# First MoE's output product by seven block products per batch in its last two groups; new urgencies

## The chip, the cores and the metric

One core of one Trainium2 chip runs the whole program as one launch. The metric is the device time of that launch in microseconds (us), the median of several runs.

## The reference

Three layers follow one another, all in float32. Shapes: batch 4, 8 heads, 576 tokens, head size 64; 2304 tokens of 512 features behind the attention.

```python
p_packed = sm_attn(p, k, v)              # 32 packed queries per batch
out = sm_attn(q, p_packed, p_packed)     # [4, 8, 576, 64] -> x [2304, 512]
h = x @ w_in                             # w_in [512, 2048]
y = (h * np.cos(h)) @ w_out              # first MoE; w_out [2048, 512]
for e in range(4):                       # second MoE; p: normalised domain_probs
    out2 += p[:, e:e+1] * (np.maximum(y @ w1[e], 0) @ w2[e])
```

The result is `out2`, [2304, 512]. Only the block `(h * cos(h)) @ w_out` is computed in another way by the change.

## The kernel before, in words

Every float32 product is made of three TensorE products of rounded halves: a value is split into `hi` (rounded, written by ScalarE) and `lo` (the rest, a subtraction on GpSimd or VectorE), and `mm3` (L235) multiplies hi·hi, hi·lo and lo·hi into one PSUM bank.

**First MoE.** The 2048 hidden features are 4 groups G of 512 (`NG = 4`), and a group is worked through batch by batch (`bb`), which makes 16 iterations. An iteration has these parts:

- `m_front` (16 narrow matmuls, L390) folds the packed keys into `w_in`; its tile `m` is split by ScalarE (L593) and VectorE (L596).
- `a_front` (four times, 12 matmuls with 288 columns each, tiles `pa<-at,m`) makes 128 hidden features of 576 tokens. h·cos(h) follows: round (ScalarE L619), remainder (VectorE L622), sine (ScalarE L626), product (VectorE L629, which frees the PSUM tile), then hi (ScalarE L633) and lo (GpSimd L636) into a tile `g`.
- `a_back` (four times, 24 matmuls with 288 columns, tiles `pa<-g,w`) multiplies 512 hidden features with 128 output features of `w_out`; VectorE adds the sum to the accumulator `yacc` in SBUF (L674 in the first group, L676 later). Behind the last group a DMA stores `yacc` (L682).

The fronts of the next batch are put between the backs of this one. PSUM holds 4 tiles `pa` of two banks in this part. Weights arrive as raw 64-bit words and are decoded ahead of use by `w_block` (VectorE L296 to L310, GpSimd L324 and L327).

**Second MoE.** Tokens are done in three passes of 512, 1024 and 768, each of 8 units (expert and half). `b_pair` already multiplies by seven block products instead of eight (tiles `pb<-bop,aop`), and `b_back`/`b_back2` the output products. `weights` loads raw weights, forms sums (L872), splits them (L736, L727) and stores them to DRAM for the later passes; `tokens` loads `y`, forms sums (L937) and splits them into `bop`. SBUF for this part is opened by gates (`f_gate1` to `f_gate4`) as the pools of the first MoE close.

**Order.** The order on every engine is set by `Plan`: each operation has an engine, a duration, what it waits for, what it holds, and a key (urgency); `run` places operations in simulated time, by earliest start and then by key. TensorE's keys, and those of some DMAs, come from the table `KEYS`. An operation with `alt` may go to VectorE instead of GpSimd. Operations marked `port` are planned one after another with those of GpSimd. All engines issue in order, so the plan is the program.

Of the kernel before, what the change touches and what calls it, by code (L numbers as in the profile page):

```python
# [163 lines left out]
def tile_packed_attention_moe_moe2(ctx: ExitStack, tc: tile.TileContext, qT, kT, vk, vr, pT, w_in, w_out, dp, w1, w2, out, out2):  # L164
# [16 lines left out]
    nc = tc.nc  # L181
# [63 lines left out]
    pl = Plan({"pa": -4, "pb": -8, "t": -5, "g": 8, "m": 2, "at": 2, "raw64": 2, "wd": 4, "T": 2, "w": 4, "yh": 8, "pz": -2,  # L245
# [13 lines left out]
    HEAD_G = 2  # L259
    wblk = {}  # L260

    def w_block(what, G, k, key, pieces=1, ld_key=None):
# [4 lines left out]
        s = {"slot": sw or sd}  # L267
# [17 lines left out]
        for p in range(pieces):  # L285
# [31 lines left out]
            def f_hi(c=c, p=p):  # L317
                if p == 0:
                    s["w"] = wo.tile([P, 2, 2, 512], F32R, tag="w", name="w", bufs=4)
                nc.scalar.activation(s["w"][:, c, 0], s["D"][:, c].bitcast(F32), AF.Copy)  # L320
# [71 lines left out]

    def attn_p(bb, keys):
# [14 lines left out]
        ready = []  # L408
        for e in range(2):
            ta, tT = pl.slot("t"), pl.slot("T")  # L410
# [9 lines left out]
            def f_exp(e=e):  # L420
                s["a", e] = x = tp.tile([P, S], F32, tag="t", name="a", bufs=5)
# [45 lines left out]
            x = pl.op("ACT", 0.813, f_exp, [b], [ta], [p1[e]], table="exp")  # L467
# [21 lines left out]
    def attn_q(bb, key, key_st):  # L489
# [13 lines left out]
        for e in range(2):  # L503
            tx, ta = pl.slot("t"), pl.slot("t")
# [33 lines left out]
            def f_xt(e=e):  # L538
                s["xt", e] = a = tp.tile([P, S], F32, tag="t", name="xt", bufs=5)
# [10 lines left out]
            a = pl.op("DVE", 0.81, f_x, [first], [tx], [p1[e]])  # L550
# [6 lines left out]
            a = pl.op("DVE", 0.77, f_xt, [a], [ta], [tx])  # L557
# [46 lines left out]
    def a_front(G, bb, i, key):  # L604
        M, so = ms[G, bb], at_slot[G, bb]
        p1, tt = pl.slot("pa"), pl.slot("t")
        s = gs[G, bb, i] = {"slot": pl.slot("g")}
# [9 lines left out]
        def f_rnd():  # L617
            s["t"] = tp.tile([P, 2, S2], F32, tag="t", name="t", bufs=5)
# [20 lines left out]
        a = pl.op("ACT", 0.652, f_rnd, [a], [tt], [p1])  # L639
        a = pl.op("DVE", 0.753, f_rem, [a], [], [p1, tt])  # L640
        a = pl.op("ACT", 0.685, f_sin, [a], [], [tt], table="sin")
        a = pl.op("DVE", 0.753, f_mul, [a], [], [p1, tt])
        a = pl.op("ACT", 0.69, f_hi, [a], [s["slot"]], [tt])
        s["ready"] = pl.op("POOL", 1.43, f_lo, [a], [], [tt, s["slot"]])

    yslot, ydone = {}, {}

    def a_back(G, bb, dm, key):
# [6 lines left out]
        last = None  # L655
        for i in range(4):
            def f_mm(i=i):
                if i == 0:
                    s["y"] = psum2()
                w, gt = wblk["out", G, i // 2]["w"], gs[G, bb, i]["g"]  # L660
                for c in range(2):
                    mm3(s["y"][:, c, :S2], lambda x: w[:, i % 2, x, dm * P:(dm + 1) * P], lambda x: gt[:, x, c], i == 0,
                        i == 3)

            wb = wblk["out", G, i // 2]
# [13 lines left out]
        def f_store():  # L679
            if bb not in y_d:  # L680
                y_d[bb] = dpool.tile([P, 4, S], F32, tag=f"y{bb}", name=f"y{bb}", bufs=1)
            nc.sync.dma_start(out=y_d[bb][:, 2 * hf:2 * hf + 2], in_=yacc[bb, hf])  # L682

        a = pl.op("DVE", 0.757, f_evac, [last, ydone.get((bb, dm))], [ysl] if G == 0 and dm % 2 == 0 else [], [p1, ysl],
                  key + 15, begun=[ydone[bb, dm - 1]] if G == 0 and dm % 2 else [])
        ydone[bb, dm] = a
# [883 lines left out]
```

## Time and profile before

| | us |
|---|---|
| median of 3 runs (1112.24 to 1116.63) | 1114.18 |
| the profiled execution | 1118.35 |
| its span, first to last instruction | 1116.6 |
| TensorE busy | 1084.9 (97%) |
| VectorE busy | 856.3 (77%) |
| GpSimd busy | 666.8 (60%) |
| ScalarE busy | 491.9 (44%) |
| DMA traffic | 247.04 MB, mean 221 GB/s |

The profile is of one execution. A matmul's busy time includes the time in which the next one is already being filled in, so a busy TensorE isn't TensorE at its peak: the steady rate is read from how long a counted row of matmuls takes. "Idle before" is the time an engine stood still just before an instruction, with what ended it. Attention and the first MoE fill the stretch up to 384.1 us, the second MoE the rest.

### The profile page before, as it was taken

How to read it: one execution, taken by the hardware profiler on the slowest of the kernel's cores; microseconds unless marked ns; L12 is line 12 of the kernel's file. 1: busy time of each engine (PE TensorE's matmuls, PEld its weight loads, DVE VectorE, ACT ScalarE, POOL GpSimd, SP SyncE). 2: the span in 40 equal slices, each digit the busy share in tenths (PEclk: the TensorE clock that was granted, in tenths of full speed). 3: DMA queues.
4: the chain of work that ended last, by engine and by line, in shares of the span. 5: the costliest groups of instructions: out<-in, count | busy, mean ns of one | idle time of the engine just before them, and what ended most of it. 6: DMA issues, size and time to landing. Idle time of an engine off the chain costs nothing.

```text
span 1116.6 us, 18619 instructions
## 1 busy us (share of the span) xinstructions
PE 1084.9 (97%) x6985; PEld 976.5 (87%) x6985; DVE 856.3 (77%) x1354; ACT 491.9 (44%) x863; POOL 666.8 (60%) x477
## 2 busy tenths in 40 slices
PE   6799999999999999999999999999999999999998
PEld 5588999999999988889888888888878899999998
DVE  4798977854456577878567788888988987788787
ACT  4777755544435345345424443333343352333331
POOL 2757765552325477756455776976577865555564
PEclk8799999999999999999999999999999999999999
DMA  9853468511135899979866745565576687767744
GB/s 365 318 193 120 168 257 291 185 43 59 72 119 178 280 362 365 327 287 348 330 235 211 226 156 184 193 207 178 166 256 213 203 300 240 233 224 234 236 148 141
DMA packets 82942, 247.04 MB, mean 221 GB/s; under 512 B 11101, under 2 KB 22181, under 8 KB 80677
## 3 DMA queue, kind: packets, MB, share of 16 engines
q1 hardware_dynamic: 82852, 245.86, 63.2%
q8 instruction: 55, 0.90, 0.3%
q14 instruction: 35, 0.28, 0.1%
HBM read 181.83 MB, written 72.39 MB: 228 GB/s over the span
## 4 chain that ended last, share of the span: by engine, by line
PE 81%; DMA 9%; DVE 4%; ACT 2%; issue 1%; POOL 1%; SPq 1%; ACTq 0%; DVEq 0%; POOLq 0%
PE pb L235 51%; PE pa L235 27%; PE pa L390 2%; DMA raw<-w 1%; DMA w<-w 1%; DMA raw<-w_out 1%; DMA qt<-qT 1%; DMA bop<-t1t 1%; DMA bop<-t2t 1%; SPq L226 1%; ACT aop L736 1%; DMA w<-w5w 1%; DMA w<-q4w 1%; DMA w<-w3w 1%; DMA a3a<-aop 1%
## 5 line engine op out<-in xcount | busy, mean ns | idle before, releaser
L235 PE MATMUL pb<-bop,aop 128*128 128x256 f32 (+2 forms) x2016 | 369.8, 337 | 7.4 <-DVE pb L1076 2.1
L235 PEld LDWEIGHTS pb<-bop,aop 128*128 128x128 f32 x2016 | 326.4, 189 | 42.0 <-DVE pb L1076 2.8
L727 POOL TENSOR_TENSOR g<-u,g 128x512 fp32r<-128x512 f32 (+1 forms) x159 | 201.0, 1281 | 135.3 <-ACT g L736 131.9
L235 PE MATMUL pb<-g,w 128*128 128x384 f32 (+1 forms) x1056 | 217.0, 355 | 4.4 <-DVE acc L1248 1.5
L235 PEld LDWEIGHTS pa<-g,w 128*128 128x128 f32 x1536 | 207.3, 188 | 12.3 <-DVE t L629 4.2
L235 PE MATMUL pa<-g,w 128*128 128x288 f32 x1536 | 215.5, 296 | 0.3 <-DVE x L512 0.3
L235 PEld LDWEIGHTS pb<-g,w 128*128 128x128 f32 x1056 | 188.4, 188 | 22.5 <-DVE acc L1248 2.8
L736 ACT ACTIVATE g<-u 128x512 fp32r<-128x512 f32 (+1 forms) x192 | 104.6, 573 | 203.9 <-DVE u L1105 155.6
L636 POOL TENSOR_TENSOR g<-t,g 128x576 fp32r<-128x576 f32 x64 | 94.6, 1500 | 98.6 <-ACT g L633 98.4
L1248 DVE TENSOR_TENSOR acc<-pb,acc 128x512 f32<-128x512 f32 (+1 forms) x148 | 91.1, 619 | 30.5 <-PE pb L235 29.4
L235 PE MATMUL pa<-at,m 128*128 128x288 f32 x768 | 111.2, 298 | 0.1
L235 PEld LDWEIGHTS pa<-at,m 128*128 128x128 f32 x768 | 105.7, 190 | 2.2 <-issue 1.0
L1076 DVE TENSOR_TENSOR pb<-pb,p 128x256 f32<-128x256 f32 (+2 forms) x144 | 78.9, 559 | 31.8 <-PE pb L235 30.9
L727 POOL TENSOR_TENSOR w<-w 128x512 fp32r<-128x512 f32 x58 | 81.9, 1424 | 29.1 <-DVE s L797 16.7
L235 PE MATMUL pb<-w,g 128*128 128x512 f32 x384 | 91.8, 390 | 0.0
L235 PEld LDWEIGHTS pb<-w,g 128*128 128x128 f32 x384 | 70.7, 188 | 13.8
L622 DVE SCALAR_TENSOR_TENSOR t<-t,pa 128x576 f32<-128x576 int32 x64 | 47.7, 750 | 42.3 <-ACT t L619 42.2
L619 ACT ACTIVATE t<-pa 128x576 int32<-128x576 f32 x64 | 40.9, 646 | 67.9 <-PE pa L235 63.7
L235 PE MATMUL pb<-g,w2s 128*128 128x512 f32 x288 | 69.2, 391 | 1.2 <-DVE w2s L727 0.6
L629 DVE TENSOR_TENSOR t<-t,pa 128x576 f32<-128x576 f32 x64 | 47.6, 749 | 23.9 <-ACT t L626 23.7
L1076 DVE TENSOR_TENSOR p<-pb,p 128x256 f32<-128x256 f32 (+2 forms) x96 | 52.5, 552 | 17.5 <-ACT p L1138 10.5
L235 PEld LDWEIGHTS pb<-g,w2s 128*128 128x128 f32 x288 | 53.5, 188 | 13.9 <-DVE w2s L727 1.1
(131 smaller groups left out, 1363.2 us busy)
## 6 DMA issues: line engine op xcount, KB each, us to landing
at<-at SPq DMA_DIRECT2D x16, 1152.0 KB, 5.3
raw<-w SPq DMA_DIRECT2D x32, 512.0 KB, 6.4
w<-w SPq DMA_DIRECT2D x64, 256.0 KB, 3.5
raw<-w_in SPq DMA_DIRECT2D x6, 1024.0 KB, 9.5
raw<-w_out SPq DMA_DIRECT2D x6, 1024.0 KB, 5.1
kt<-kT SPq DMA_DIRECT2D x8, 576.0 KB, 9.5
qt<-qT SPq DMA_DIRECT2D x8, 576.0 KB, 9.7
y<-yacc SPq DMA_DIRECT2D x8, 576.0 KB, 2.8
```

What stands on the lines that cost most here:

```text
L226: nc.sync.dma_start(out=dst, in_=src)
L235: nc.tensor.matmul(o, lhsT=l(a), rhs=r(b), start=first and i == 0, stop=last and i == 2, skip_group_check=True)
L390: nc.tensor.matmul(o(e)[32 * q:32 * q + 32, :N], lhsT=l[64 * e:64 * e + 64, 32 * q:32 * q + 32], rhs=r(q // 2, q % 2)[64 * e:64 * e + 64], ...
L619: nc.scalar.activation(s["t"].bitcast(I32), s["u"][:, :, :S2], AF.Copy, bias=0.25)
L622: nc.vector.scalar_tensor_tensor(out=s["t"], in0=s["t"].bitcast(I32), scalar=-0.25, in1=s["u"][:, :, :S2], op0=ALU.add, op1=ALU.subtract)
L629: nc.vector.tensor_tensor(out=s["t"], in0=s["t"], in1=s["u"][:, :, :S2], op=ALU.mult)
L636: nc.gpsimd.tensor_tensor(out=s["g"][:, 1], in0=s["t"], in1=s["g"][:, 0].bitcast(F32), op=ALU.subtract)
L727: (nc.vector if on_vector else nc.gpsimd).tensor_tensor(out=dst[:, 1], in0=src, in1=dst[:, 0].bitcast(F32), op=ALU.subtract)
L736: nc.scalar.activation(r["t"][:, 0], src(), AF.Copy)
L1076: nc.vector.tensor_tensor(out=s[o] if o in s else tmp(o), in0=s[x], in1=s[y], op=ALU.add)
L1248: nc.vector.tensor_tensor(out=o, in0=o if how == ALU.subtract else p, in1=p if how == ALU.subtract else o, op=how)
```

## The change

For the groups G = 2 and 3 and all batches but the last batch of group 3 (`seven(G, bb)`, seven of the 16 iterations), the four `a_back` calls are replaced by `a_strassen`: the 512x512 block of `w_out` and the 512x576 block of hidden values are each taken as 2x2 blocks, and the product is made of seven block products instead of eight. For these:

- `a_front` ends at the product (L629); `a_blocks` then forms four differences `total` of hidden values on VectorE and makes hi and lo of seven blocks (ScalarE; GpSimd or VectorE) instead of four.
- `w_sums` forms four sums of the weights per group (VectorE) and splits them into tiles `ws` (3 buffers), two of `w_out`'s eight quarters less in `w_block`. In the last group the quarter a21, which the last batch's four plain backs need, is kept in DRAM (`a21_d`) and loaded again into a `ws` tile.
- `a_strassen` holds up to three PSUM tiles a, b, c; a bank is added to after it has been read, and seven reads (`evac`, VectorE) add to `yacc` instead of four.
- Temporaries of fronts and attention come in pairs ("t" has 4 buffers of double size instead of 5). Of the second MoE's `bop` tiles t3 moves from the pool of gate 2 to that of gate 4, b21 from gate 4 to gate 3.
- The planner's DMA costs in the second MoE are raised (0.26 to 0.3, 0.52 to 0.61, tokens by 1.25); `KEYS` has new numbers throughout and a part of its own for the third pass (`three`).

```diff
@@ a_front @@
+        s["mul"] = a = pl.op("DVE", 0.753, f_mul, [a], [], [p1, tt])
+        if seven(G, bb):
+            return
@@ a_blocks @@
+        def block(x, p, after, y):
...
+            a = pl.op("ACT", 0.69, f_hi, after, [s["slot"]], [y["ts"]])
+            s["ready"] = pl.op("POOL", 1.43, f_lo, [a], [], [y["ts"], s["slot"]], alt=0.745)
...
+        def total(o, a, b, after, use):
+            def f_sum():
+                nc.vector.tensor_tensor(out=o(), in0=a(), in1=b(), op=ALU.subtract)
...
+        t3 = total(part(d, 1), part(e, 1), part(d, 1), got + [T["sum1"]], [d, e])
+        block("b22", part(e, 1), got, e)
+        t2 = total(part(e, 1), part(e, 1), part(d, 0), got + [T["sum1"], t3, T["b22"]["ready"]], [d, e])
...
@@ a_strassen @@
+        s, slots, done = {}, {x: pl.slot("pa") for x in "abc"}, {}
...
+                p = pl.op("PE", 0.809, f_mm, A[a]["ready"] + [T[b]["ready"]] + ([] if new else [done[bank]]),
...
+        step("a11", "b11", "a", [(0, 0)], keys[0])
+        step("s1", "t1", "b", [(1, 1)], keys[1])
+        step("s2", "t2", "a", [(0, 1)], keys[2])
+        step("s4", "b22", "b", [(0, 1)], keys[3])
+        step("s3", "t3", "a", [(1, 1)], keys[4])
+        step("a12", "b21", "c", [(0, 0)], keys[5])
+        step("a22", "t4", "a", [(1, 0)], keys[6])
@@ KEYS @@
-            'f': [[-1763.8, -1743, -1713.5, -1305.2], [-260.3, -242.8, -236.8, -344.4], [14.6, 71.8, -10.1, 111.3],
+            'f': [[-1930.5, -1912, -1473.7, -1461], [-140.7, -135.8, -352.1, -174.9], [-51.4, 2.1, 47.2, 135.1],
...
```

How the order moves, at three places (names left of the arrow are written, right of it read).

TensorE, one iteration of group 3 from one `m_front` to the next, before:

```order
L390 MATMUL pa<-wd,ptf 32x512 x8
L235 MATMUL pa<-g,w 128x288 x24
L235 MATMUL pa<-at,m 128x288 x12
L235 MATMUL pa<-g,w 128x288 x24
L235 MATMUL pa<-at,m 128x288 x24
L235 MATMUL pa<-g,w 128x288 x24
L235 MATMUL pa<-at,m 128x288 x12
L235 MATMUL pa<-g,w 128x288 x24
```

and such an iteration in the change (`ws` are the weight sums; s1 lies in a `w` tile):

```order
L235 MATMUL pa<-g,ws 128x288 x12
L235 MATMUL pa<-g,w 128x288 x12
L235 MATMUL pa<-at,m 128x288 x12
L235 MATMUL pa<-g,w 128x288 x12
L235 MATMUL pa<-at,m 128x288 x12
L235 MATMUL pa<-g,ws 128x288 x12
L235 MATMUL pa<-at,m 128x288 x12
L235 MATMUL pa<-g,w 128x288 x12
L235 MATMUL pa<-at,m 128x288 x12
L235 MATMUL pa<-g,ws 128x288 x12
L235 MATMUL pa<-g,w 128x288 x12
L400 MATMUL pa<-wd,ptf 32x512 x8
```

The output product falls from 96 matmuls to 84 and is cut into pieces of 12, with a front between most of them.

VectorE, the same place before, all that stands between two `m` splits (L596):

```order
L676 SCALAR_TENSOR_TENSOR yacc<-pa,yacc 128x576
L622 SCALAR_TENSOR_TENSOR t<-t,pa 128x576
L629 TENSOR_TENSOR t<-t,pa 128x576
L676 SCALAR_TENSOR_TENSOR yacc<-pa,yacc 128x576
L622 SCALAR_TENSOR_TENSOR t<-t,pa 128x576
L629 TENSOR_TENSOR t<-t,pa 128x576
L622 SCALAR_TENSOR_TENSOR t<-t,pa 128x576
L676 SCALAR_TENSOR_TENSOR yacc<-pa,yacc 128x576
L629 TENSOR_TENSOR t<-t,pa 128x576
L622 SCALAR_TENSOR_TENSOR t<-t,pa 128x576
L676 SCALAR_TENSOR_TENSOR yacc<-pa,yacc 128x576
L629 TENSOR_TENSOR t<-t,pa 128x576
```

and the first 12 of the 18 rows between two `m` splits in the change (L812 `evac`, L699 `total`, L926 `lo`, L653 and L660 the fronts):

```order
L812 SCALAR_TENSOR_TENSOR yacc<-pa,yacc 128x2x288 x2
L699 TENSOR_TENSOR t<-t 128x2x288
L653 SCALAR_TENSOR_TENSOR t<-t,pa 128x576
L812 SCALAR_TENSOR_TENSOR yacc<-pa,yacc 128x2x288
L926 TENSOR_TENSOR g<-t,g 128x576
L660 TENSOR_TENSOR t<-t,pa 128x576
L653 SCALAR_TENSOR_TENSOR t<-t,pa 128x576
L812 SCALAR_TENSOR_TENSOR yacc<-pa,yacc 128x2x288
L699 TENSOR_TENSOR t<-t 128x2x288
L660 TENSOR_TENSOR t<-t,pa 128x576
L653 SCALAR_TENSOR_TENSOR t<-t,pa 128x576
L812 SCALAR_TENSOR_TENSOR yacc<-pa,yacc 128x2x288
```

VectorE has some 20 instructions per iteration in place of 13 with the `m` split, 4 of them with both inputs in SBUF.

The DMA queue (SyncE), behind the last load of `at`, before:

```order
L226 DMA raw<-w 128x2x512 x4
L682 DMA y_3876<-yacc 128x1152 x2
L226 DMA ys<-y_3876 128x2x256 x4
L682 DMA y_4076<-yacc 128x1152
L748 DMA a0a_4090<-aop 128x1024
L226 DMA raw<-w 128x2x512
L748 DMA a0s_4105<-aop 128x1024
```

and in the change:

```order
L843 DMA y_3811<-yacc 128x1152 x2
L226 DMA raw<-w 128x2x512 x4
L226 DMA ys<-y_3811 128x2x256 x4
L843 DMA y_4046<-yacc 128x1152 x2
L947 DMA a0a_4145<-aop 128x1024
L226 DMA raw<-w 128x2x512
L947 DMA a0s_4169<-aop 128x1024
L226 DMA ws<-a_116 128x2x256
```

The first raw weights of the second MoE now stand behind the stores of batch 0 instead of ahead of them, and the reload of a21 (`ws<-a_116`) stands behind the store of a split weight sum.

## Rows read from the trace of the kernel before

**Rows 1.** Head of the page: span, then busy us (share) and instructions by engine.
```profile
span 1116.6 us, 18619 instructions
...
PE 1084.9 (97%) x6985; PEld 976.5 (87%) x6985; DVE 856.3 (77%) x1354; ACT 491.9 (44%) x863; POOL 666.8 (60%) x477
```

**Rows 2.** The page's chain that ended last, share of the span by engine.
```profile
PE 81%; DMA 9%; DVE 4%; ACT 2%; issue 1%; POOL 1%; SPq 1%; ACTq 0%; DVEq 0%; POOLq 0%
```

**Rows 3.** Busy time by stretch; then granted clock, DMA share, GB/s.
```profile
core 0: us, PE busy (x) PEld busy (x) DVE busy (x) ACT busy (x) POOL busy (x), PEclk, DMA share, GB/s
0.00:105.00 105.00, 90.05 (x1066) 73.55 (x1067) 79.00 (x159) 70.10 (x109) 58.67 (x49) 0.89 0.66 252
...
203.50:325.90 122.40, 122.40 (x972) 116.32 (x961) 69.39 (x90) 55.75 (x83) 47.38 (x31) 1.00 0.25 88
325.90:384.10 58.20, 58.19 (x442) 57.58 (x432) 37.05 (x46) 21.20 (x36) 24.72 (x17) 1.00 0.57 203
384.10:556.00 171.90, 165.94 (x1031) 148.70 (x1032) 131.73 (x230) 78.80 (x173) 110.12 (x74) 1.00 0.92 332
556.00:821.00 265.00, 264.55 (x1167) 217.88 (x1167) 215.95 (x318) 102.29 (x173) 178.68 (x127) 1.00 0.60 199
821.00:1116.60 295.60, 285.33 (x1549) 269.91 (x1547) 242.68 (x412) 103.10 (x202) 181.73 (x147) 1.00 0.66 220
```

**Rows 4.** The chain in order of time, 300 to 390: start us, us, what.
```profile
305.96 19.37 PE pa L235 x144
325.32 1.02 PE pa L390 x16
326.34 57.76 PE pa L235 x432
...
384.13 0.77 DVE yacc L676
```

**Rows 5.** VectorE's groups in 203.5 to 325.9: xcount | busy us, mean ns | idle before.
```profile
L676 DVE SCALAR_TENSOR_TENSOR yacc<-pa,yacc 128x576 f32<-128x576 f32 x25 | 18.8, 753 | 6.8 <-PE pa L235 6.8
L629 DVE TENSOR_TENSOR t<-t,pa 128x576 f32<-128x576 f32 x24 | 18.1, 752 | 14.8 <-ACT t L626 14.8
L622 DVE SCALAR_TENSOR_TENSOR t<-t,pa 128x576 f32<-128x576 int32 x24 | 18.0, 752 | 27.0 <-ACT t L619 27.0
L596 DVE TENSOR_TENSOR m<-pa,m 128x1024 fp32r<-128x1024 f32 x6 | 7.3, 1220 | 4.2 <-ACT m L593 4.2
```

**Rows 6.** GpSimd's and ScalarE's groups of the same stretch.
```profile
L636 POOL TENSOR_TENSOR g<-t,g 128x576 fp32r<-128x576 f32 x26 | 36.9, 1441 | 71.4 <-ACT g L633 71.4
...
L633 ACT ACTIVATE g<-t 128x576 fp32r<-128x576 f32 x24 | 15.1, 676 | 4.2 <-DVE t L629 4.2
```

**Rows 7.** VectorE's group of token sums in 325.9 to 384.1.
```profile
L937 DVE TENSOR_TENSOR ys<-ys 128x512 f32<-128x512 f32 x4 | 3.8, 960 | 1.8 <-DMA ys<-y 1.8
```

**Rows 8.** VectorE in order of time, 325 to 390: two of those token sums.
```profile
349.84 0.69 DVE L937 TENSOR_TENSOR ys<-ys 128x512 f32<-128x512 f32 x1
...
373.40 1.77 DVE L937 TENSOR_TENSOR ys<-ys 128x512 f32<-128x512 f32 x1
```

**Rows 9.** The DMA queue in order of time, 318 to 400: start us, us.
```profile
317.81 9.00 SPq L226 DMA_DIRECT2D raw<-w  x4
336.16 6.22 SPq L682 DMA_DIRECT2D y<-yacc  x2
344.83 1.91 SPq L226 DMA_DIRECT2D ys<-y  x4
```

**Rows 10.** The page's DMA issues: KB each, median us from issue to landing.
```profile
w<-w SPq DMA_DIRECT2D x64, 256.0 KB, 3.5
```

**Rows 11.** TensorE in order of time, 0 to 60, with idle before.
```profile
35.63 1.12 PE L429 MATMUL pa<-ident,a 128*128 128x128 f32 x4 [3.95 <-ACT a L423]
```

**Rows 12.** ScalarE in order of time, 10 to 60, ahead of that wait.
```profile
30.90 0.68 ACT L294 ACTIVATE dt<-raw 128x512 f32<-128x512 f32 x1
...
34.74 0.74 ACT L423 ACTIVATE a<-pa,nb 128x576 f32<-128x576 f32 x1
```

More of the change, by code (lines that the diff above doesn't have):

```diff
@@ L259, in tile_packed_attention_moe_moe2, with seven @@
     HEAD_G = 2
+    GS = 2
+    def seven(G, bb):
+        return G >= GS and (G, bb) != (NG - 1, B - 1)
     wblk = {}
@@ L266, in w_block @@
         sw = pl.slot("w") if what == "out" else None
-        s = {"slot": sw or sd}
+        s = {"slot": sw or sd, "dslot": sd, "key": key}
+        half = what == "out" and G >= GS and k == 0
         head = G < HEAD_G
@@ L605, in a_front @@
         M, so = ms[G, bb], at_slot[G, bb]
-        p1, tt = pl.slot("pa"), pl.slot("t")
-        s = gs[G, bb, i] = {"slot": pl.slot("g")}
+        p1 = pl.slot("pa")
+        s = gs[G, bb, i] = {}
+        even = gs[G, bb, i - i % 2]
+        tt = s["ts"] = even["ts"] if i % 2 else pl.slot("t")
+        if not seven(G, bb):
+            s["slot"] = pl.slot("g")
         def f_mm():
@@ L648, in a_back, with y_store, f_store @@
+    def y_store(bb, hf, after, key):
+        def f_store():
+            if bb not in y_d:
+                y_d[bb] = dpool.tile([P, 4, S], F32, tag=f"y{bb}", name=f"y{bb}", bufs=1)
+            nc.sync.dma_start(out=y_d[bb][:, 2 * hf:2 * hf + 2], in_=yacc[bb, hf])
+        y_done[bb, hf] = dma(0.59 * MB, f_store, after, [], [yslot[bb, hf]], key + 50, base=TO_DRAM)
     def a_back(G, bb, dm, key):
@@ L677, in f_evac @@
                                                op1=ALU.add)
[L679 to L686, printed above, removed]
+        a = pl.op("DVE", 0.757, f_evac, [last] + [ydone.get((bb, dm, c)) for c in range(2)], [ysl] if G == 0 and dm % 2 == 0 else [], [p1, ysl],
+                  key + 15, begun=[ydone[bb, dm - 1, 0]] if G == 0 and dm % 2 else [])
+        ydone[bb, dm, 0] = ydone[bb, dm, 1] = a
         if G == NG - 1 and dm % 2:
-            y_done[bb, hf] = dma(0.59 * MB, f_store, [ydone[bb, dm - 1], a], [], [ysl], key + 50, base=TO_DRAM)
+            y_store(bb, hf, [ydone[bb, dm - 1, 0], a], key)
     def spans(h, j):
@@ L1408, in at @@
             l = KEYS[what]
+            if what in ("m", "f") and its[n][0] >= GS:
+                return l[-2 + (n == len(its) - 1)]
+            if what == "b" and n == len(its) - 1:
+                return l[-1]
+            if what in ("m", "f", "b"):
+                l = l[:-1 if what == "b" else -2]
             return l[n] if n < len(l) - 1 else l[-1]
@@ L1419, in tile_packed_attention_moe_moe2 @@
             w_block(what, G + 1, bb % 2, k0 + at("blk", n))
+            if bb == 3 and G + 1 >= GS:
+                w_sums(G + 1)
         if n + 2 < len(its):
@@ L1426, in tile_packed_attention_moe_moe2 @@
                 a_front(*its[n + 1], i, k0 + at("f", n + 1)[i])
+                if i % 2 and seven(*its[n + 1]):
+                    a_blocks(*its[n + 1], i // 2)
+        if seven(G, bb):
+            a_strassen(G, bb, [k0 + x for x in KEYS["s"]])
+            continue
         for i in range(4):
@@ L1470, in tile_packed_attention_moe_moe2 @@
     pl.late = 0.3
-    late = [o for o in ops_a if o["f"].__qualname__.split(".")[-3] in ("a_front", "a_back")]
+    LATE = ("a_front", "a_back", "block", "total", "prod", "evac", "w_halves", "y_store", "w_sums")
+    late = [o for o in ops_a if o["f"].__qualname__.split(".")[-3] in LATE]
     mid = [o for o in ops_a if o["f"].__name__ == "f_mm" and "a_front" in o["f"].__qualname__]
@@ L1492, in tile_packed_attention_moe_moe2 @@
         k0 = 100 * len(its) + 100 * n
-        place = KEYS["first"] if n == 0 else KEYS["one"] if h == 0 else KEYS["end"] if n >= NSTEP - 1 else KEYS["two"]
+        place = KEYS["first"] if n == 0 else KEYS["one"] if h == 0 else KEYS["end"] if n >= NSTEP - 1 else KEYS["two" if h == 1 else "three"]
         if n > NU:
-            b_back2(n - 1, Ws.pop(n - 1), [k0 + x for x in KEYS["last" if n == NSTEP else "two" if n < NSTEP - 1 else "end"]["b"]])
+            b_back2(n - 1, Ws.pop(n - 1), [k0 + x for x in KEYS["last" if n == NSTEP else "end" if n == NSTEP - 1 else "two" if n <= 2 * NU else "three"]["b"]])
         elif n > 0:
```

263 lines of the change are left out of this document (183 added, 80 removed), and 33 rows, old and new, of the table KEYS.

## The prediction

> **What bounds the kernel now.** I read the head of the page first: TensorE is busy for 1084.9 of 1116.6 us, VectorE for 77%, GpSimd for 60% [rows 1]; the chain that ended last runs through TensorE for 81% of the span [rows 2]. These are averages over unlike stages, so the next view is busy time by stretch [rows 3]. Between 203.5 and 384.1 us, where groups 2 and 3 of the first MoE lie, TensorE never stands still, VectorE is busy for 69.39 of 122.40 us and DMA has a share of 0.25. From 384.1 to 556 us (the second MoE's first pass) TensorE still stands still only 6 us, but DMA's share is 0.92. In the third pass, from 821 us, TensorE is idle for 295.6 - 285.3 = 10.3 us, and at the head of the program for 105 - 90 = 15 us.
>
> The chain in order of time gives TensorE's steady rate [rows 4]: 144 counted matmuls in 19.37 us, 134.5 ns each, then 1.02 us of `m_front`. An iteration takes 20.4 us, and the chain leaves TensorE only at 384.13 us. So in this stage a matmul saved is time saved, as long as the other engines keep up.
>
> **The change, part by part.**
>
> *Matmuls.* A batch's output product falls from 96 to 84 matmuls (7 products x 2 output halves x 2 x 3), in 7 batches: 84 fewer, and nothing else is taken from TensorE or given to it. 84 x 134.5 ns = **11.3 us less** [rows 4]. An iteration then needs 132 x 134.5 ns + 1.02 us = 18.8 us of TensorE.
>
> *What VectorE has to do meanwhile.* Before, an iteration asks of it four remainders and four products at 752 ns, four evacuations at 753 ns and one `m` split at 1220 ns [rows 5]: 6.0 + 3.0 + 1.2 = 10.2 us of 20.4. The change makes that 6.0 + 7 x 0.753 + 1.2 = 12.5 us, and adds four `total`s and, by the order, about one `lo` per batch. Neither shows in the trace of before at this size; the nearest row is a token sum, also two float32 inputs from SBUF, with 512 columns in place of 576. It took 0.69 us at its best and 1.77 us at its worst [rows 8], 0.96 on average [rows 7]. For 576 columns that makes 0.78, 1.99 and 1.08 us. Five such instructions: 5.4 us (3.9 to 10.0). So VectorE needs **17.9 us of 18.8** per iteration, at least 16.4, at most 22.5. I take the mean, since it comes from a stretch where GpSimd was about as busy as it will be here (24.72 of 58.2 us [rows 3]; here some six `lo` at 1.44 us [rows 6], 8.6 of 18.8).
>
> The rows say that the same sum can take 2.5 times as long. The Trainium skill (SBUF — State Buffer, "Who interferes with whom") has a rule that speaks against this change: VectorE with two SBUF inputs and GpSimd reading SBUF exclude each other for the whole instruction, so one of the two waits for the other to end. The spread in rows 8 agrees. By the rule a `total` that always came second would cost its own time and a whole `lo`; the sum below, by the row's mean, has it come second about every third time.
>
> *What that does to TensorE.* On 95% of VectorE each front's PSUM tile is held longer, and a bank a or b can only be added to after VectorE has read it; one front of 12 matmuls (1.6 us) stands between the two, against 0.75 us for the read and its wait in VectorE's queue. Before, VectorE had idle time ahead of nearly every one of its reads [rows 5]; that cover goes. I charge 0.5 us per iteration, a little over half of one queued instruction: 7 x 0.5 = **3.5 us more** (0 if all is hidden; at the far end VectorE sets the pace, below).
>
> *ScalarE and GpSimd.* Three more hi at 676 ns per batch bring ScalarE from 55.75 of 122.4 us to about 11 of 18.8 per iteration [rows 3, 6]; GpSimd gets two or three more `lo` at 1.44 us and stays near half. Both are covered. `w_sums` (eight sums, once per group) is work of one iteration that has four others to spread over: nothing, at worst 8 x 1.1 = 9 us of VectorE that it would have to find in the spare 0.9 us of several iterations; part of the 3.5.
>
> *The reload of a21.* It stands in the DMA queue behind a store that waits for a split. Between the last product that reads a sum of this group and the first that needs a21 there are 72 matmuls, 9.7 us. A 256 KB load took 3.5 us to land [rows 10]; hi and lo add 0.7 + 1.4 us. Covered with 4 us to spare; without the cover 5.6 us. I charge nothing.
>
> *The start of the second MoE.* Its raw loads, sums and first operands were made behind the last 58.2 us of the first MoE: raw loads from 317.81 us, first store of `y` at 336.16, token loads at 344.83 [rows 9]. In the change's order 288 matmuls follow the last `m_front`: 38.7 us. In 58.2 us VectorE was busy for 37.05 and DMA for a share of 0.57 [rows 3]. The same DMA work in 38.7 us would be a share of 0.86, which the next stretch exceeds (0.92), so it fits, tightly; VectorE, with more reads in it, doesn't quite. Bounds: 0, or all of 58.2 - 38.7 = 19.5 us late. The store of batch 0, from which the tokens come, moves only by the products behind it (three fewer us of 48), so I stay close to the lower end: **2 us more**.
>
> *Head of the program.* TensorE waits 3.95 us for the second batch's softmax [rows 11], while ScalarE decodes weights ahead of it [rows 12]. The new order decodes them before the `m` split, where ScalarE waited for TensorE. **1 us less**; anything from 4 less (the whole wait) to 4 more (another one as long).
>
> *New urgencies in the second MoE.* No count changes there. What better keys can win is idle time: 10.3 us in the third pass, which gets keys of its own, and 6 in the first [rows 3]. What they can lose is as much as one of these again. Part of the idle is data dependence at the joints of passes, so I take **3 us less** (10 less to 6 more).
>
> Sum: -11.3 + 3.5 + 2 - 1 - 3 = -9.8 us. The profiled execution took 1118.35 us, so 1108.5 for one like it; the runs' median, 1114.18, lies 4.2 us lower, and from it the forecast is **1104.4 us**.
>
> **The rivals.**
>
> 1. *VectorE becomes the bound of the seven iterations (slower).* If every `total` and `lo` is stretched as the worst token sum was, an iteration takes 22.5 us in place of 18.8: 7 x 3.7 = 26 us, less the 11.3 saved: 1129 us. It decides from the point where VectorE needs the 20.4 us of before, that is where these five instructions average 1.6 us. For it: 1.77 us was seen once [rows 8]. Against: the mean is far below. This is the skill's rule about the shared port at its full price. 0.08.
> 2. *The gain is spent at the joint (no change).* DMA is the limit of the first pass (0.92, 332 GB/s [rows 3]) and its work can't begin before the last `m_front`. If DMA moves 203 GB/s in the shorter window too, 19.5 us x 203 GB/s = 4.0 MB are left over, and at 332 GB/s they take 12 us: the 11.3 us are gone, 1114 us. For it: that share, and VectorE close to full in the same window. Against: TensorE stood still for only 6 us in that pass. 0.20.
> 3. *The new keys close most of the gaps.* -11.3 + 1 - 2 - 8 = -20 us: 1094 us. For it: 16 us of idle in the first and third pass. Against: those gaps are many, small, and end on different engines. 0.12.
>
> That leaves 0.60 for the forecast. That TensorE would not be relieved at all isn't a rival: the order has exactly 84 matmuls fewer.
>
> **How the numbers follow.** About 0.5% (5.6 us) is what a measurement of this kernel can tell from no change, so faster means under 1108.6 us. The forecast's own range, from its terms (0 to 7 for the stage, 0 to 5 for the joint, 6 less to 3 more for keys and head), is 1097 to 1113; a little of it, some 0.04 of the 0.60, ends above 1108.6. Faster: 0.56 + 0.12 + a few hundredths of rival 2, where the joint only eats half, = 0.72. Slower by over 0.5%: 0.08. The same: 0.20. The range reaches down to rival 3's middle and up past rival 2's: 1094 to 1115 us.
>
> **What would show it.** In the profile after: 1452 matmuls `pa` of output products in place of 1536; iterations of groups 2 and 3 of 18.8 us plus at most half a microsecond; VectorE at 90 to 97% in that stretch and `total` at a mean near 1.1 us; GpSimd's `lo` at 1.4 to 1.6 us. Waits of TensorE on L812 or on the fronts' L660 in the dozens of nanoseconds speak for the forecast, one of a microsecond in each iteration for rival 1. The first product of the second MoE about 8 us earlier than at 385 us, and no more than 8 us idle in the first pass, speak against rival 2. Wrong would be: an iteration above 20 us; a wait on the a21 tile; a first pass longer than its 172 us by more than 5.

## The result, and the profile after

The median fell from 1114.91 us (4 runs) to **1103.15 us** (4 runs, 1099.91 to 1106.27): a ratio of 0.9896, 95% interval 0.986 to 0.9933. That is 11.8 us less; forecast were 9.8 less (1104.4 us, range 1094 to 1115). The profiled execution took 1104.06 us, 0.9 above the median; the one of before lay 3.4 us above its own, so the two traced executions differ by some 2.5 us more than the medians do, and their spans (1116.6 and 1101.3 us) by 3.5.

The head of the page and the chain by engine of the kernel after, which answer to [rows 1, 2]:

```profile
span 1101.3 us, 18549 instructions
...
PE 1069.6 (97%) x6901; PEld 963.0 (87%) x6901; DVE 905.2 (82%) x1414; ACT 510.7 (46%) x893; POOL 703.4 (64%) x504
...
PE 80%; DMA 7%; DVE 6%; ACT 2%; POOL 2%; issue 2%; SPq 0%; POOLq 0%; ACTq 0%; DVEq 0%
```

6901 matmuls in place of 6985: exactly 84 fewer. VectorE gained 49 us of work, GpSimd 37. Busy time by stretch answers to [rows 3]. Up to the start of the first pass the borders lie at the same places of the program as there; the later ones don't (the first pass ends at 562.0 us before and at 544.4 here):

```profile
core 0: us, PE busy (x) PEld busy (x) DVE busy (x) ACT busy (x) POOL busy (x), PEclk, DMA share, GB/s
0.00:105.00 105.00, 86.21 (x1058) 69.95 (x1059) 77.09 (x156) 70.03 (x109) 58.83 (x48) 0.89 0.65 252
105.00:214.60 109.60, 108.42 (x848) 102.99 (x846) 87.29 (x116) 64.19 (x97) 68.65 (x40) 1.00 0.62 218
214.60:337.10 122.50, 121.57 (x954) 114.84 (x953) 110.31 (x142) 68.63 (x108) 72.44 (x46) 1.00 0.25 89
337.10:376.90 39.80, 39.59 (x304) 38.53 (x304) 35.24 (x45) 19.15 (x32) 27.65 (x19) 1.00 0.69 246
376.90:544.40 167.50, 166.35 (x1048) 150.73 (x1047) 133.14 (x237) 82.73 (x178) 110.33 (x75) 1.00 0.96 358
544.40:821.80 277.40, 276.75 (x1220) 228.38 (x1219) 229.34 (x336) 107.34 (x181) 188.42 (x134) 1.00 0.60 202
821.80:1101.30 279.50, 270.70 (x1482) 257.55 (x1481) 232.78 (x385) 98.67 (x191) 177.10 (x146) 1.00 0.65 217
```

The stage that was 57% full on VectorE is 90% full (110.31 of 122.50), and TensorE still stands still there for under 1 us. The surprise is in the first pass of the second MoE. Between its own borders the kernel before shows

```profile
385.03:562.05 177.02, 171.54 (x1057) 152.97 (x1058) 133.41 (x233) 83.65 (x180) 115.73 (x77) 1.00 0.92 334
```

so DMA's share rose from 0.92 to 0.96 and 334 GB/s to 358, and TensorE's idle time fell from 5.5 to 1.2 us.

The chain in order of time answers to [rows 4]; `x132` is what an iteration of seven products has:

```profile
283.32 17.76 PE pa L235 x132
301.08 1.02 PE pa L400 x16
...
357.74 19.47 PE pa L235 x144
377.21 11.53 PE pb L235 x96
```

17.76 + 1.02 = 18.8 us per iteration, as worked out. `aop`, `bop` and the last evacuation are ready when TensorE gets there: nothing stands between the last `pa` matmul and the first `pb`, where before it waited for VectorE [rows 4]. Five marks of TensorE's timeline split the difference:

| us | before | after | stage shorter by |
|---|---|---|---|
| first front starts | 42.1 | 40.7 | 1.4 (head) |
| second MoE's first product starts | 385.0 | 377.0 | 6.6 (first MoE) |
| last product of 256 columns ends | 562.0 | 544.4 | 9.6 (first pass) |
| first product of 384 columns starts | 844.7 | 828.6 | -1.5 |
| end of the span | 1116.6 | 1101.3 | -0.9 (third pass) |

Not all of the 9.6 us is won. Ahead of the last product of 256 columns stand 385 matmuls of 512 columns in the kernel before and 373 in the change. The other twelve, some 0.23 us each (in the change 30 such matmuls take 6.97 us from 821.62 us on), have only moved behind the mark: 2.8 us, which the next row pays. Like for like the first pass got 6.9 us shorter: 4.3 us of idle time, and the rest in the matmuls beside TensorE's stops, whose time counts as busy.

So the first MoE explains 6.6 of the 15.3 us between the traces; about as much came from a pass in which no product was added or removed.

VectorE's and GpSimd's groups in the iterations of seven products (239.8 to 337.1), which answer to [rows 5, 6] (L812 `evac`, L699 `total`, L926 `lo`):

```profile
L812 DVE SCALAR_TENSOR_TENSOR yacc<-pa,yacc 128x576 f32<-128x576 f32 x34 | 25.5, 752 | 4.3 <-PE pa L235 3.8
L699 DVE TENSOR_TENSOR t<-t 128x576 f32<-128x576 f32 x22 | 17.2, 784 | 2.0 <-POOL g L926 1.7
L653 DVE SCALAR_TENSOR_TENSOR t<-t,pa 128x576 f32<-128x576 int32 x20 | 14.9, 745 | 2.4 <-ACT t L650 2.4
...
L926 DVE TENSOR_TENSOR g<-t,g 128x576 fp32r<-128x576 f32 x6 | 8.1, 1358 | 0.7 <-ACT g L689 0.6
```

```profile
L926 POOL TENSOR_TENSOR g<-t,g 128x576 fp32r<-128x576 f32 x32 | 49.8, 1572 | 35.8 <-ACT g L689 28.6 <-issue 2.6 <-PE pa L235 2.4
```

A `total` takes 784 ns, at the lower end of the bounds (780 to 1990). GpSimd's `lo` takes 1572 ns in place of 1441, and the six `lo` on VectorE 1358 ns each, where the prediction counted 1080: what waiting there was shows in the `lo` more than in the `total`. TensorE's waits in the first MoE after its head are short and few; the longest, at 189 us, lies ahead of the first seven products:

```profile
PE pa L235 <- DVE t L660: 1.2, 1, 1.2
PE pa L235 <- DVE yacc L812: 0.5, 2, 0.3
PE pa L235 <- POOL g L926: 0.4, 1, 0.4
PE pa L235 <- ACT aop L935: 0.2, 1, 0.2
```

### The profile page after: what moved, and what is told of

The parts are those of the page before. It is cut to its first block, busy times and chain, and to the rows that moved or that the text cites. A ratio compares the mean times of both kernels' runs of the same rounds, so it can differ in the third digit from the quotient of the medians.

```text
span 1101.3 us, 18549 instructions
## 1 busy us (share of the span) xinstructions
PE 1069.6 (97%) x6901; PEld 963.0 (87%) x6901; DVE 905.2 (82%) x1414; ACT 510.7 (46%) x893; POOL 703.4 (64%) x504
## 4 chain that ended last, share of the span: by engine, by line
PE 80%; DMA 7%; DVE 6%; ACT 2%; POOL 2%; issue 2%; SPq 0%; POOLq 0%; ACTq 0%; DVEq 0%
PE pb L235 57%; PE pa L235 21%; DMA raw<-w_out 2%; PE pa L400 1%; DMA raw<-w 1%; DVE u L1304 1%; DMA qt<-qT 1%; DVE acc L1447 1%; DMA raw<-w_in 1%; POOL g L926 1%; DMA w<-w 1%; POOL g L667 1%; DMA w<-w2w 1%; DVE g L926 1%; DMA w<-w1w 1%
## 5 line engine op out<-in xcount | busy, mean ns | idle before, releaser
L926 POOL TENSOR_TENSOR g<-u,g 128x512 fp32r<-128x512 f32 (+1 forms) x163 | 204.4, 1270 | 131.5 <-ACT g L935 127.6
L235 PE MATMUL pa<-g,w 128*128 128x288 f32 x1176 | 168.1, 296 | 1.5 <-POOL g L667 1.2
L235 PEld LDWEIGHTS pa<-g,w 128*128 128x128 f32 x1176 | 159.4, 188 | 11.2 <-issue 4.7
L926 POOL TENSOR_TENSOR w<-w 128x512 fp32r<-128x512 f32 x62 | 87.4, 1423 | 24.7 <-DVE s L996 13.3
L926 POOL TENSOR_TENSOR g<-t,g 128x576 fp32r<-128x576 f32 x42 | 64.2, 1545 | 55.4 <-ACT g L689 48.2
L667 POOL TENSOR_TENSOR g<-t,g 128x576 fp32r<-128x576 f32 x36 | 55.0, 1548 | 16.5 <-ACT g L664 16.5
L1293 DVE SCALAR_TENSOR_TENSOR u<-pb,ys 128x512 f32<-128x512 f32 (+1 forms) x96 | 58.8, 617 | 5.4 <-PE pb L235 3.5
L1304 DVE TENSOR_TENSOR u<-p,u 128x512 f32<-128x512 f32 (+1 forms) x64 | 62.2, 981 | 0.1
```

The costliest lines, as they stand in the source:

```text
L235: nc.tensor.matmul(o, lhsT=l(a), rhs=r(b), start=first and i == 0, stop=last and i == 2, skip_group_check=True)
L667: nc.gpsimd.tensor_tensor(out=s["g"][:, 1], in0=s["t"], in1=s["g"][:, 0].bitcast(F32), op=ALU.subtract)
L926: (nc.vector if on_vector else nc.gpsimd).tensor_tensor(out=dst[:, 1], in0=src, in1=dst[:, 0].bitcast(F32), op=ALU.subtract)
L1293: nc.vector.scalar_tensor_tensor(out=o, in0=s[src], scalar=0.0, in1=share["t"][:, half], op0=ALU.max, op1=ALU.mult)
L1304: nc.vector.tensor_tensor(out=o, in0=U[a]["t"], in1=U[b]["t"], op=ALU.subtract)
```

## The experiments

All but the last (e4) are the changed kernel with one edit; each was also profiled. "First product" is that of the second MoE, "first pass" runs from it to the end of the last product of 256 columns, "third" from the first product of 384 columns to the end of the span (us).

| run | median | ratio to before, 95% interval | first product | first pass | third |
|---|---|---|---|---|---|
| before (its one trace) | 1114.9 | 1 | 385.0 | 177.0 | 271.8 |
| the change | 1103.15 | 0.9896 (0.986, 0.9933) | 377.0 | 167.4 | 272.7 |
| e10, 84 matmuls put back | 1113.6 | 0.9977 (0.9967, 0.9987) | 386.7 | 166.6 | 273.7 |
| e1, eight products | 1135.8 | 1.0179 (1.0145, 1.0213) | 393.5 | 182.6 | 272.9 |
| e6, seven in group 3 alone | 1132.7 | 1.017 (1.0133, 1.0207) | 389.8 | 182.9 | 274.1 |
| e7, seven in group 1 too | 1154.6 | 1.0338 (1.0315, 1.036) | 426.9 | 167.1 | 274.8 |
| e5, doubled `total` | 1122.9 | 1.0051 (1.0029, 1.0072) | 393.9 | 166.8 | 273.0 |
| e13, reductions added | 1117.4 | 1.0015 (0.9997, 1.0034) | 388.8 | 167.1 | 271.8 |
| e14, all `lo` on GpSimd | 1102.9 | 0.9891 (0.9867, 0.9914) | 378.4 | 166.7 | 272.3 |
| e2, old urgencies, second MoE | 1119.9 | 1.0038 (1.0017, 1.006) | 383.8 | 180.6 | 271.3 |
| e12, old ones, first pass | 1135.5 | 1.0168 (1.0147, 1.0189) | 376.5 | 170.8 | 282.8 |
| e9, no own urgencies in third | 1107.0 | 0.992 (0.9894, 0.9946) | 374.7 | 167.2 | 277.5 |
| e3, old DMA costs | 1125.8 | 1.0091 (1.0065, 1.0116) | 376.8 | 190.0 | 272.7 |
| e4, kernel before with new urgencies and costs | 1121.4 | 1.0043 (1.0027, 1.0059) | 389.7 | 170.5 | 275.0 |

The first pass's mark hasn't the same work ahead of it in every run: 385 matmuls of 512 columns before and in e2, 349 in e12, 373 in all others. From the first product to the first one of 384 columns, where the work is the same, it took 459.7 us before, 451.5 in the change and 454.6 in e4.

### What are 84 matmuls worth? (e1, e6, e10)

```diff
-    GS = 2
+    GS = 4
```

> The changed kernel with GS = 4, so that all 16 batches take the four plain backs (96 matmuls) and no weight sums are made; pools, planner costs and the table of urgencies stay new. Theory (the matmuls make the gain ahead of the second MoE, the urgencies the gain behind it): the second MoE's first product comes 11.3 us later less the 3.5 us that the stage now loses, near 385 us as before; from there to the end 724 us as in the changed kernel, not 731.5 as before; about 1110 us in all. Rival (the seven products bring nothing once VectorE's and the new waits are paid, all comes from new urgencies): within 3 us of the changed kernel's 1103.

It took 1135.8 us, 20 us more than the kernel before: neither theory. The urgencies were found for the plan with seven products; with another one the work at the joint of the two MoEs comes late. TensorE's waits from 355 to 430 us:

```profile
PE pb L235 <- ACT aop L935: 6.8, 2, 4.5
PE pa L235 <- POOL g L667: 4.1, 1, 4.1
PE pa L235 <- DVE t L660: 1.6, 1, 1.6
```

With `GS = 3`:

> The changed kernel with GS = 3: seven products in group 3 alone, 3 batches in place of 7, 48 matmuls more. Theory (each batch of seven is worth 12 matmuls, 1.6 us, and urgencies suit it as they stand): 4 x 1.6 = 6.5 us slower, 1110. Rival (urgencies only suit the plan that they were found for): over 10 us slower, with the loss at the start of the second MoE, as in the run with eight products everywhere (33 us).

1132.7 us, the rival, with the same waits on ScalarE's `aop` (6.7 us). Both runs plan anew, so neither prices a matmul. A price needs an edit of which the plan knows nothing:

```diff
-                    for j in range(2):
+                    for j in (0, 1, 0, 1) if bank == "c" else (0, 1):
```

> The changed kernel with the product a12 x b21 done twice in each of the seven batches: 12 more matmuls per batch, 84 in all, as many as the change removed; the second set starts its PSUM bank anew, so values stay. The plan doesn't know of it, the order stays. Theory (a matmul saved in this stage is time saved, at 134.5 ns): 11.3 us slower than the changed kernel, all of it before the second MoE's first product (377 -> 388), about 1114. Rival (other engines share the bound there, VectorE above all): the longer iteration (20.4 us) gives them room, so only part of it comes back, 4 to 8 us, 1107 to 1111.

The first product came at 386.7 us, 9.6 later; the median is 1113.6, 10.5 more (by the two ratios to before 0.81%, 9.0 us). Two iterations of the changed kernel by stretch, then the same two here:

```profile
262.80:282.20 19.40, 18.99 (x149) 17.79 (x148) 18.05 (x25) 9.80 (x16) 11.15 (x7) 1.00 0.18 61
282.20:301.00 18.80, 18.80 (x149) 17.78 (x148) 16.70 (x24) 12.01 (x20) 10.76 (x8) 1.00 0.17 56
```

```profile
262.80:283.85 21.05, 20.64 (x161) 19.41 (x160) 18.09 (x25) 9.84 (x17) 11.15 (x7) 1.00 0.17 59
283.85:304.25 20.40, 20.40 (x163) 19.39 (x162) 16.70 (x24) 11.99 (x20) 10.78 (x8) 1.00 0.15 49
```

Each is 1.6 us longer, the time of 12 matmuls, and so is the one before them (24.60 in place of 23.00 us): nothing hides, not even in the iterations in which TensorE waits for late halves. From the `m_front` ahead of the seven iterations (at 214.6 us in the changed kernel, at 213.0 in e10) to the first product it took 162.4 and 173.7 us. So 84 matmuls are worth 11.2 us there, all of the 11.3. That the first product comes only 9.6 us later is due to the stretch ahead, where both kernels have the same instructions: the changed kernel's trace has the wait of 1.2 us at 189 us, e10's has not.

With these matmuls back, the rest of the change is worth 0.23% (0.13 to 0.33): 2.6 us by this ratio, 1.75 by the medians (1115.35 before, among the same runs).

### Is VectorE the next bound? (e5, e13, e14, e7)

```diff
                 nc.vector.tensor_tensor(out=o(), in0=a(), in1=b(), op=ALU.subtract)
+                nc.vector.tensor_tensor(out=o(), in0=o(), in1=o(), op=ALU.max)
```

> The changed kernel with each difference of hidden values (28 in all) followed by one more VectorE instruction of the same size and kind, an element-wise maximum of the tile with itself, which leaves the values as they are; the plan doesn't know of it, so the order stays. Theory (VectorE, busy for 16.7 of 18.8 us per iteration, is next to be the bound): four more at 0.78 us make 19.8 us, so each of seven iterations loses about 1 us and some queueing, 7 to 12 us in all, 1110 to 1115. Rival (the prediction's size, 17.9 us plus four at 1.08): 22.2 us per iteration, 24 us in all, 1127. Rival (there is slack enough, latency is hidden by the order): under 3 us.

The first product came 16.9 us later: between the theory and the prediction's size. By stretch, one row per iteration:

```profile
265.50:287.10 21.60, 19.36 (x151) 17.89 (x150) 20.93 (x29) 10.66 (x17) 11.03 (x7) 1.00 0.19 71
287.10:308.40 21.30, 19.49 (x149) 17.85 (x148) 19.39 (x29) 11.62 (x20) 10.70 (x7) 1.00 0.16 53
308.40:332.20 23.80, 21.13 (x150) 19.39 (x149) 21.61 (x27) 11.95 (x20) 14.12 (x10) 0.93 0.15 56
```

VectorE is at 91 to 97% (third number), and each iteration takes 2.5 to 5 us more than 18.8. In the third one the granted clock, 0.93, adds to it. So the spare that VectorE has is about 2 us per iteration (18.8 - 16.7). Four more instructions cost more than the 11.8 us that the change won; three would have used it up, by an estimate in proportion (12.7 us). Rival 1 was that near.

The same with an instruction that reads one operand (its output tile is left out here):

```diff
...
+                nc.vector.tensor_reduce(out=junk, in_=o(), op=ALU.max, axis=AX.XY)
```

> As the run with doubled differences, but the 28 added VectorE instructions are reductions (maximum over the tile into one column that nobody reads): one input in SBUF in place of two, of nearly the same length; order and values stay. In the run with two inputs the second MoE's first product came at 393.9 us in place of 377.1, 16.9 us later. Theory (VectorE and GpSimd shut each other out when VectorE reads two operands from SBUF, and that is a good part of the loss): 5 to 10 us later in place of 16.9, GpSimd's lo no longer than the 1.57 us of the changed kernel. Rival (only VectorE's own time counts): 14 to 18 us later again.

11.7 us later, between the two. 28 reductions of 753 ns are 2.8 us shorter than 28 second differences of 853. But of those the shortest took 757 ns, so these 2.8 us are waiting too. The two runs lie 5.2 us apart, and e5 lost some 2 us of that in the iteration with the lower clock; that leaves some 3 us, and at most the 5.2, for the shared access. GpSimd's `lo` took 1552 ns here against 1628 in e5:

```profile
L928 POOL TENSOR_TENSOR g<-t,g 128x576 fp32r<-128x576 f32 x34 | 52.2, 1552 | 47.0 <-ACT g L690 35.5 <-PE pa L236 5.1 <-issue 4.1
```

```profile
L927 POOL TENSOR_TENSOR g<-t,g 128x576 fp32r<-128x576 f32 x32 | 51.5, 1628 | 46.9 <-ACT g L689 35.0 <-issue 6.1 <-PE pa L235 5.8
```

Two operands from SBUF do lengthen the other engine's instruction, here by some 5%; most of what the added instructions cost, 11.7 of 16.9 us, is their own time on VectorE.

```diff
-                split(s["g"], p(), v)
+                split(s["g"], p(), False)
```

> The changed kernel with the seven lo of hidden blocks that the plan gives to VectorE issued on GpSimd instead, at the same place in the plan. VectorE loses 1.36 us per iteration (16.7 -> 15.4), GpSimd gets one more lo of 1.57. Theory (VectorE is the tighter of the two): the stage gets up to 1.5 us faster, 1101.5 to 1103. Rival (the plan gave them to VectorE because GpSimd was behind there, and products wait for them): 2 to 8 us slower, TensorE waiting on GpSimd's lo.

1102.9 us: no difference that can be told. VectorE didn't get the 1.36 us back either: in two iterations it is busy for 16.0 and 16.6 us, since `total` takes 890 ns there in place of 784. Neither engine stops TensorE as the kernel stands, so moving a `lo` between them moves nothing.

With `GS = 1`:

> The changed kernel with GS = 1: seven products in group 1 too, 11 batches in place of 7, 48 matmuls fewer. Theory (matmuls count only while VectorE keeps up; in group 1 it also decodes weights, busy for 15 to 18 of 20.4 us per iteration in the kernel before, and would need 6 us more): VectorE is the bound there, 2 to 4 us lost per iteration against 1.6 won: 2 to 10 us slower than the changed kernel, 1105 to 1113. Rival (decoding can move to where VectorE has time): 6.5 us faster, 1096.6.

1154.6 us, far worse than either: the theory named the place, but neither the size nor the cause. Iterations of group 1 took 34 to 38 us. By stretch:

```profile
134.30:169.15 34.85, 27.96 (x197) 25.62 (x196) 29.57 (x34) 17.64 (x26) 24.11 (x15) 0.94 0.41 151
169.15:207.50 38.35, 26.62 (x180) 22.86 (x182) 28.17 (x34) 15.01 (x21) 19.17 (x11) 0.86 0.57 197
207.50:241.50 34.00, 23.77 (x156) 20.54 (x158) 24.55 (x33) 11.66 (x17) 14.26 (x8) 0.80 0.66 220
```

VectorE isn't full (72 to 85%); products wait for ScalarE's and GpSimd's halves (22.4 and 10.2 us between 120 and 330), and the clock falls to 0.80 on top. What made these halves late wasn't traced further, and how much of this a search for urgencies could win back was not tried.

### Where do the first pass's 9.6 us come from? (e2, e12, e9, e3, e4)

> The changed kernel with the urgencies of the second MoE (first, one, two, end, last, keep, kept, later, g, copy) taken from the kernel before, and those of two for the third pass too; seven products, pools and planner costs stay. Theory (new urgencies make the 7 us that the second MoE got shorter): from its first product to the end about 731 us in place of 724, first pass longer by 6 to 8 us; 1110 us in all. Rival (the pools' new order, later loads and raised DMA costs make it, not the keys): 724 us stays, 1103 in all. A worse result than either, above 1115, would say that keys are only good for the plan that they were found with.

1119.9 us. From the first product to the end it took 733.6 us in place of 724.3, near what the theory had (with the first pass 13 us longer, 10.5 like for like). But the first product also came 6.7 us later. For 3.0 of these TensorE waited for a load of the first MoE: all eight copies of `w2` (`copy`) stand ahead of it in the DMA queue, in the changed kernel three of the eight:

```profile
PE pa L235 <- DMA at<-at: 3.0, 1, 3.0
```

> The changed kernel with only those urgencies of the kernel before that rule the second MoE's first pass (first, one, keep, kept, g); all of the first MoE and the later passes keep the new ones. Theory (new urgencies of the first pass make the 7 us by which the second MoE got shorter): first product still near 377 us, from it to the end 731 to 734 us in place of 724, 1110 to 1113 in all. Rival (the later start of its loads, the other homes of its operands, or the third pass make it): under 2 us longer, 1103 to 1105.

1135.5 us, far above both. The first product came as without the edit (376.5), and from there to the end it took 33 us more. The first pass has 3.4 of them, 9 like for like (with 24 matmuls of 512 columns fewer ahead of its mark); the others come behind it. The edit reaches there too: among the urgencies put back is `g`, which rules sums (L1304) that stand in the second and third pass alone (from 568 us on in the changed kernel). From 848 to 860 us GpSimd is full, TensorE half idle, and its clock at 0.78:

```profile
848.00:860.00 12.00, 6.15 (x26) 5.08 (x26) 10.00 (x10) 0.63 (x1) 12.00 (x8) 0.78 0.22 88
```

So this run didn't edit the first pass alone. It tells that a part of the table can't be put back by itself, and not where the gain lies.

> The changed kernel with the third pass ruled by the second pass's urgencies, as in the kernel before, in place of its own. The prediction's term (own urgencies win 3 us in the third pass): third pass, from its first product to the end, 3 us longer than 272.7 us, 1106 in all. Rival (it was 271.8 us before and 272.7 after, so they bring nothing): within 1.5 us of the changed kernel, 1102 to 1104.

1107.0 us, third pass 277.5 us: the prediction's term in its size (3.8 us by the medians, 4.7 in the trace). But this compares with the new urgencies of the second pass, and against the kernel before the third pass is no shorter (272.7 against 271.8). The own part only makes good what the others took.

```diff
-            r["raw"] = dma(0.3 * MB2, f, after, [r["slot"]])
+            r["raw"] = dma(0.26 * MB2, f, after, [r["slot"]])
...
-                ld[what, k] = dma(0.61 * MB2, f_load(what, k), [gate[1]], [sr[what, k]])
+                ld[what, k] = dma(0.52 * MB2, f_load(what, k), [gate[1]], [sr[what, k]])
```

(and the tokens' 1.25 taken back)

> The changed kernel with the planner's DMA costs of before in the second MoE (0.26, 0.52, tokens by 1) and the new urgencies. Theory (the costs hold loads where the chip has them, and the first pass's gain rests on them together with the urgencies): first pass (first product to the last product of 256 columns, 167.4 us in the changed kernel, 177.0 before) 3 to 8 us longer. Rival (the urgencies alone make it): within 2 us of 167.4.

First pass 190.0 us, 22.6 more: far beyond the theory's 3 to 8. These numbers are in no instruction, they only tell the planner how long a transfer takes, and with them it puts token loads for later passes ahead of raw weights. The DMA queue of this run,

```profile
394.77 1.92 SPq L226 DMA_DIRECT2D ys<-y  x3
396.79 0.41 SPq L947 DMA_DIRECT2D q0w<-w2s  x1
...
401.49 3.74 SPq L226 DMA_DIRECT2D ys<-y  x3
...
407.61 1.54 SPq L226 DMA_DIRECT2D raw<-w  x2
```

and at the same time in the changed kernel, where raw weights go first and the tokens after (by 404 us four loads of raw weights since the first product, in e3 two):

```profile
393.05 0.38 SPq L226 DMA_DIRECT2D raw<-w  x1
...
400.68 0.91 SPq L226 DMA_DIRECT2D raw<-w  x1
...
403.66 4.28 SPq L226 DMA_DIRECT2D ys<-y  x4
```

TensorE then waits 6.4 us at once for the split of a weight sum (L1071). On VectorE that sum stands behind a token sum for the third pass, which itself waits for a transfer:

```profile
403.74 1.65 DVE L1175 TENSOR_TENSOR ys<-ys 128x768 f32<-128x768 f32 x1 [4.05 <-DMA t1t<-ys]
```

After it TensorE goes on at a lower clock. By stretch, e3 and then the changed kernel:

```profile
400.00:424.00 24.00, 15.42 (x96) 14.02 (x96) 18.35 (x25) 8.66 (x20) 15.45 (x11) 0.86 1.04 399
```

```profile
400.00:424.00 24.00, 23.17 (x161) 21.52 (x160) 19.24 (x40) 10.52 (x25) 17.96 (x12) 1.00 1.01 380
```

DMA is full in both. What differs is the order, of the bytes and of what waits for them. That the old costs are worse by themselves isn't shown: here they go with urgencies that came with the new ones.

The last run has nothing of the seven products, pairs or moved operands, only urgencies and costs, in the kernel before:

> The kernel before with the second MoE's new urgencies and raised DMA costs, and nothing else of the change. Theory (these are better for any plan): 7 us faster than before, 1107 to 1109. Rival (urgencies only suit the plan in which they were found; they are ranks among what else is ready): no faster, and slower by 5 to 20 us, with the waits at the start of the second MoE, where loads and splits compete.

The rival came true: 6 us slower. Yet the first pass took 170.5 us in place of 177.0, like for like 3.7 us less (2.8 are the twelve matmuls moved), so the new urgencies with the new costs make about half of its 6.9 us without any other part of the change; what makes the other half isn't shown. The run is slower in all, since at the joint TensorE waits for evacuations:

```profile
PE pb L235 <- DVE yacc L676: 3.1, 1, 3.1
PE pa L235 <- DVE yacc L676: 2.0, 1, 2.0
```

The last of them stand on VectorE behind a token sum that waits 7.75 us for its transfer (in the kernel before its first such wait is 3.5 us):

```profile
385.78 1.22 DVE L976 TENSOR_TENSOR ys<-ys 128x1024 f32<-128x1024 f32 x1 [7.75 <-DMA ys<-y]
```

The first product comes 4.7 us later than before, and the third pass takes 3.1 more.

No run of these beat the changed kernel by more than its interval.

## Why the prediction was right, and where it was not

The total was right (9.8 us less forecast, 11.8 measured), and so was its largest term, the matmuls, in mechanism and size. The smaller terms were not. By the traces stage waits, joint and urgencies came out 8.6 us better than forecast, and 2.7 us were lost between 52 and 214 us, where the prediction charged nothing. That the sum lies so near the medians is in part luck.

- **84 matmuls, 11.3 us.** The count was exact, and so was the iteration of 18.8 us. e10 prices them at 11.2 us in the stretch where they stand, and at 9.0 to 10.5 by whole executions.
- **Stage waits, 3.5 us more.** Right in kind, too large. From 214.6 us to the first product it took 162.4 us; 1140 matmuls at 134.5 ns and seven `m_front` make 160.5. That is 1.9 us of stops, 1.7 of them in two iterations (239.8 to 282.2 us) and not 0.5 in each; e10 has the same 1.9. The whole first MoE, first front to first product, takes 346.0 us in e10 with its 96 matmuls and took 342.9 before. The rest of these 3.1 us lies ahead of the first seven products.
- **VectorE at 17.9 of 18.8 us.** 16.7 (16.70 of 18.80 in one iteration). The step that failed is the duration of a `total`, 1.08 us from a stretch with GpSimd as busy; it measured 0.78 (and a `lo` on VectorE 1.36). The rule of the Trainium skill (SBUF — State Buffer, "Who interferes with whom") agrees in kind: GpSimd's `lo` grew by 131 ns, and by another 56 in e5. Most of the bill went to GpSimd, which had time. The prediction's "about every third time" doesn't follow from its row: 0.30 us above the best is a fifth of a `lo` of 1.44.
- **The reload of a21, nothing.** No wait, as forecast, but not with 4 us to spare. Its `lo` stood behind others in GpSimd's queue and ran from 368.9 to 370.7 us, and TensorE came to the first product with this tile at 370.65.
- **The joint, 2 us more.** Wrong. From the last front's end to the first product it was 22.7 us for 168 matmuls, 22.6 at the steady rate: no wait to speak of, where before there was 0.9 us. The step that failed took the shorter cover for a loss. DMA moved 246 GB/s in it in place of 203 (0.69 share). That is some 2 MB less than in the longer window of before, so not all of the old work fitted, but nothing that the first product needs was late. Rival 2 fell with it: DMA in the first pass could be pressed from 334 to 358 GB/s.
- **Head, 1 us less.** The first front starts 1.4 us earlier, but not by the step that was named. The wait for the second batch's softmax grew from 3.95 to 5.03 us, and the transposes behind it start 0.2 us later; the front was put ahead of some matmuls of attention. At the next `m_front` 0.6 us are left (52.64 and 52.02 us).

```profile
35.80 1.12 PE L446 MATMUL pa<-ident,a 128*128 128x128 f32 x4 [5.03 <-ACT a L440]
```

- **Urgencies, 3 us less in the second MoE.** Right in sign, too small by the traces: 7.3 us less (731.5 to 724.3 from the first product to the end), all of it ahead of the third pass, which got 0.9 us longer in spite of keys of its own. The step that failed took part of the idle time (10.3 us in the third pass, 6 in the first) for data dependence that no key can win: in the first pass nearly all of it went, and in the third none.

The forecast's own range has a slip: its upper terms (7, 5 and 3 us against 11.3) make 1118 us, not 1113. Nothing hung on it.

Rival 1 is the one that the runs came closest to: four more VectorE instructions per iteration (e5) make the kernel slower than before.

What the change won besides the matmuls is 1.75 to 2.6 us by e10's many executions, and 6.5 us by the two traces (1118.35 and 1111.9). The traced execution of before lies 3.0 us above the median of the runs beside e10, and e10's 1.7 below its own; that is the difference. So how the second MoE's gain divides among its passes rests on one trace of before, and is uncertain by some 3 us.

## What to carry to other kernels

Where one engine never waits, count the instructions taken from it and check that the next busiest one keeps some room: with 2.1 of 18.8 us free the count held to 0.1 us, and with four more instructions per iteration the gain was gone. Where order comes from a planner, its durations are as much a part of the program as the code: other transfer costs under the same urgencies cost 22 us, more than the arithmetic saved. In e3 and e4 it went the same way: a token sum that waited for a transfer held up on VectorE what TensorE needed. And an edit that makes such a planner plan anew measures the plan; to price an instruction, add or remove it behind the planner's back.

## What was not expected of the hardware

TensorE's granted clock fell soon after short stops. In e5 a wait of 2.1 us within a stretch of 4 us in which it was busy for 1.86 was followed by 4.2 us at a mean of 0.69 of full speed (2.4 GHz; the level below is 1.2):

```profile
324.00:328.00 4.00, 1.86 (x12) 1.65 (x11) 3.97 (x7) 2.45 (x4) 2.37 (x2) 0.90 0.43 138
328.00:332.20 4.20, 4.20 (x24) 3.98 (x22) 3.25 (x5) 2.11 (x4) 2.79 (x2) 0.69 0.39 160
```

So a wait can cost more than its length; in e7, e12 and e3 this shows at 0.78 to 0.86 over tens of microseconds. And DMA moved 380 to 399 GB/s over 24 us with loads and stores mixed, beyond the 332 that the prediction took for its limit.
